# The filter of a Fourier mixing layer: loaded in pair order as float32 and cast in place, instead of permuted by matmuls

## Chip, core and metric

The kernel runs on one core of one Trainium2 chip. The metric is the device time of one execution in microseconds (us), the median of three runs. Engines are named as in the profile: PE is the matrix engine, DVE the vector engine, ACT the scalar engine, POOL the general-purpose engine (GpSimd), and SP the engine that only issues transfers. A transfer can be put on a queue by SP, by ACT or by POOL. An engine executes its own instructions in order, and waits on semaphores that other engines and transfers raise.

## What is computed

```python
X = np.fft.rfft(x, axis=1)                       # x: 8 x 3008 x 256, float32
Y = X * (filt_r + 1j * filt_i)[None]             # filters: 1505 x 256
y = np.fft.irfft(Y, n=3008, axis=1).astype(np.float32)
h = np.maximum(y.reshape(-1, 256) @ w_in, 0.0)   # w_in: 256 x 2048
out = (h * h) @ w_out                            # w_out: 2048 x 256
```

A global filter along the sequence (Fourier transform, product with a complex filter, transform back) is followed by a feed-forward layer with squared ReLU on all 24064 tokens.

## The kernel before

The transform of length 3008 is split as 64 x 47, and every step of it is a product with a constant matrix. For one batch the steps are these.

- `unit_a` (for batch 0: `chunk_a0`, L366, and `turn_u`, L388) is the transform of length 47. Batch 0 takes its rows from three wide loads `xw` (L228), cast to float16 by DVE and POOL.
- `unit_b` (L411) is the transform of length 64. It makes two columns of frequencies (`c`) at a time with the constant `sSB`, and DVE multiplies the bank by the filter: one instruction gives the product with the real and with the imaginary filter, `sF[:, v, c]` with v = 0 and 1 (L425). There are 12 such products for a batch, p = 0 to 11, and product p uses columns 2p and 2p + 1.
- `unit_p` (batch 0: `unit_p0`, L438) goes back over the 64 with the constant `sSP`, and, for batch 0, with `sSPx`, which is `sSP` with its halves of partitions swapped (POOL, L773 and L774). ACT moves the bank to `ze`, and SP writes it to `dZ` in DRAM.
- `read_z` (L476) reads it back in another order as `zt`, and `unit_y` (L484) finishes the inverse transform and leaves `yt`.
- `ffn_g1` (L512), `ffn_sq`, and `products` and `sums` (L602, L632) are the feed-forward layer, in 47 groups of 512 tokens with 8 slots each. From the first group on, the transforms of batches 1 to 7 are put in these slots by a plan written out by hand (`fft_plan`, L669). What comes ahead of the first slot is the prologue: it brings batch 0 to `yt`, and batch 1 through `unit_a`.

`sF` has 128 partitions. Partition f of column c holds frequency 47 f + c for f < 32, and 47 (f - 32) + 47 - c for f of 32 to 63; partitions 64 to 127 repeat this, with the sign changed for the imaginary filter. The kernel before loads each filter as 128 rows of 3008 numbers (`load_f`, L234), casts them to float16 in `f16` (L755 on POOL; L763 on DVE, POOL and ACT) and lets PE permute them: `place_f` (L269) multiplies slices of `f16` by 0-1 matrices `sPF` (108 matmuls in all, L284 and L287) into PSUM, and ACT copies each four columns into `sF` (L295). The last frequency is loaded apart (`nyq`, L248). Calls of `place_f` stand between the calls of `unit_b` (L780 to L789).

Each engine's order is the order of the program text. PSUM is in three rings of two buffers: `psH` (two banks each), `psF` and `psO`. In the prologue, `turn_u` and `place_f` rotate over all of them (`bank_pair`, L169).

Transfers in the prologue, in the order of SP's queue: the three `xw`, `filt_r`, `sPF`, `filt_i`, a small constant `sC1`, the two halves of `sSB` and `sSP`, seven pieces of `w_in` (`load_win`, L304), the six `dZ` writes and the first `zt` reads. POOL's queue carries the eight loads of batch 1's `x` (`load_x`, L186, which casts to float16 on the way), and `w_out` in two halves (`load_wout`, L320): the first half after the loads of `x`, the second half after the first `zt` has landed (L793). A new transfer takes one of eight semaphores in turn, and its issue waits until the transfer eight places earlier has landed.

Of the kernel before, what the change touches and what calls it, by code (L numbers as in the profile page):

```python
# [9 lines left out]
F16 = mybir.dt.float16  # L10
# [9 lines left out]
TG = 512  # L20
SLOTS = 8
CLS = 376
QF = 3008
PQ = ((0, 0), (0, 1), (0, 2), (1, 2), (1, 3), (1, 0))


def _build_consts():
# [23 lines left out]
    for c in range(NC):  # L51
        for j in range(32):
            freq[c, j] = 47 * j + c
            if c:
                freq[c, 32 + j] = 47 * j + 47 - c
    freq[0, 32] = N // 2


    SB = np.zeros((NM, 2, 2, NC, 2, 64))
# [3 lines left out]
    for c in range(NC):  # L63
        for f in range(64):
            k = freq[c, f]
            if k < 0:
                continue
            sg = 1.0 if (f < 32 or c == 0) else -1.0
            for h in range(2):
                th = 2 * np.pi * ((k * (32 * h + m)) % N) / N  # L70
                SB[:, h, 0, c, 0, f] = np.cos(th)
                SB[:, h, 1, c, 0, f] = -sg * np.sin(th)
                SB[:, h, 0, c, 1, f] = -np.sin(th)
                SB[:, h, 1, c, 1, f] = -sg * np.cos(th)
            if c == 0 and f == 32:
                SB[:, :, 1, c, :, f] = 0.0
            w = (1.0 if k in (0, N // 2) else 2.0) / N
            for i in range(2):
                th = 2 * np.pi * ((k * (n1j + i)) % N) / N
                cs, sn = w * np.cos(th), w * np.sin(th)  # L80
                SP[0, f, c, i, 0] = cs
                SP[0, f, c, i, 1] = sg * sn
                SP[1, f, c, i, 0] = -sn
                SP[1, f, c, i, 1] = sg * cs
# [7 lines left out]
            SY[c + c // 12 * 4, i, 1, :, i] = -np.sin(th)  # L92


    PF = np.zeros((128, 6, 2, 2, 32))
    for w, (s, q) in enumerate(PQ):
        for j in range(32):
            PF[4 * j + q, w, :, s, j] = 1.0

    f16 = lambda a, p: np.ascontiguousarray(a.reshape(p, -1).astype(np.float16))  # L100
    C0 = np.zeros((128, 896))
    C0[:, 0:576] = S0.reshape(128, 6, 2, 2, NC).transpose(0, 1, 4, 2, 3).reshape(128, 576)
# [1 line left out]
    for h in range(2):  # L104
        C0[64 * h:64 * h + N2, 704:752] = SA[:, h, h].reshape(N2, 48)
    C0[:, 768:862] = SY.reshape(128, 94)
    return f16(C0, 128), f16(PF, 128), f16(SB, 128), f16(SP, 128)


@with_exitstack  # L110
def kernel(
# [16 lines left out]
    NG = T // TG  # L128
    assert NG * TG == T

    C0_np, PF_np, SB_np, SP_np = _build_consts()
    dPF = nc.inline_tensor(PF_np, name="cPF")
    dC0 = nc.inline_tensor(C0_np, name="cC0")
    dSB = nc.inline_tensor(SB_np, name="cSB")
    dSP = nc.inline_tensor(SP_np, name="cSP")
# [27 lines left out]
    def psH(name):  # L163
        return pps.tile([128, 2, 512], F32, tag="psH", name=name, bufs=2)
# [37 lines left out]
    sSA = sC1[:, 0:64]  # L202
    sSY = sC1[0:112, 64:158]
    ident = sC0[:, 576:704]
    sPF = p_out.tile([128, 6, 128], F16, tag="ost", name="sPF")

    xw32, xw16 = {}, {}

# [20 lines left out]
        load_wide(k)  # L229


    f32s = []

    def load_f(im):  # L234
        filt = filt_i if im else filt_r
        t = p_y.tile([128, QF], F32, tag="yt", name=f"f32_{im}")
        nc.sync.dma_start(out=t, in_=filt[0:1504, :].rearrange("a d -> (a d)")
                          .rearrange("(p e) -> p e", e=QF))
        f32s.append(t)

    load_f(0)
    nc.sync.dma_start(out=sPF, in_=dPF.ap().rearrange("p (w q) -> p w q", q=128))
    load_f(1)
    nc.sync.dma_start(out=sC1, in_=dC0.ap()[:, 704:896])
    nyq = p_out.tile([128, 2, D], F32, tag="ost", name="nyq")
    nc.gpsimd.memset(nyq, 0.0)
    for im, filt in enumerate((filt_r, filt_i)):
        nc.gpsimd.dma_start(out=nyq[0:1, im, :], in_=filt[1504:1505, :])  # L248
    sSB = const.tile([128, NC, 128], F16, name="sSB")
    sSP = const.tile([128, NC, 128], F16, name="sSP")  # L250
    sign = const.tile([128, 1], F32, name="sign")
    nc.vector.memset(sign[0:64], 1.0)
    nc.vector.memset(sign[64:128], -1.0)


    zero = const.tile([128, 128], F16, name="zero")
    nc.vector.memset(zero, 0.0)

    nc.scalar.copy(out=zero[0:1, 0:1], in_=zero[0:1, 1:2])

    sF = const.tile([128, 2, NC, D], F16, name="sF")
    nc.vector.memset(sF[:, 0, 0:2, :], 0.0)
    ps = psO("warm").rearrange("p a d -> p (a d)")
    for _ in range(26):
        nc.tensor.matmul(ps, zero, sF[:, 0, 0:2, :], start=True, stop=True)  # L265

    f16s = []

    def place_f(im, k, *engs, rotate=False):  # L269

        if rotate:
            banks, groups = bank_pair(f"psf_{im}_{k}")
        else:
            t = psH(f"psf_{im}_{k}")
            banks, groups = [t[:, 0, :], t[:, 1, :]], [(t, 0)]
        for i in range(4):
            c = 4 * k + i
            e0, e1 = D * c, D * (47 - c)
            cuts = [0] + [d for d in range(1, D)
                          if (e0 + d) % QF == 0 or (c and (e1 + d) % QF == 0)] + [D]  # L280
            for d0, d1 in zip(cuts, cuts[1:]):
                o = banks[i // 2][:, (i % 2) * D + d0:(i % 2) * D + d1]
                q, a = divmod(e0 + d0, QF)
                nc.tensor.matmul(o, sPF[:, PQ.index((0, q)), :], f16s[0][:, im, a:a + d1 - d0],  # L284
                                 start=True, stop=False)
                q, a = divmod(e1 + d0, QF) if c else (0, QF + d0)
                nc.tensor.matmul(o, sPF[:, PQ.index((1, q)), :], f16s[0][:, im, a:a + d1 - d0],  # L287
                                 start=False, stop=True)
        for t, i in groups:
            n = t.shape[1]  # L290
            eng = engs[i % len(engs)]
            dst = sF[:, im, 4 * k + 2 * i:4 * k + 2 * i + 2 * n, :]
            src = t.rearrange("p t (a d) -> p (t a) d", d=D)
            if eng is nc.scalar:
                eng.activation(out=dst, in_=src, func=AF.Copy, scale=sign[:, 0:1] if im else 1.0)  # L295
            elif im:
                eng.tensor_scalar_mul(out=dst, in0=src, scalar1=sign[:, 0:1])
            else:
                eng.tensor_copy(out=dst, in_=src)

    sWin = const.tile([128, 2, DFF], F16, name="sWin")
    sWout = const.tile([128, NJT, 256], F16, name="sWout")
# [84 lines left out]

    def turn_u(k, eng):  # L388

        banks, groups = bank_pair(f"psT_{k}")  # L390
# [345 lines left out]
    for k in range(3):  # L736
        cast_wide(k, nc.vector, nc.gpsimd if k == 2 else nc.vector)

    def load_const(t, d, k):
        c = slice(12 * k, 12 * k + 12)  # L740
        nc.sync.dma_start(out=t, in_=d.ap().rearrange("p (a b) -> p a b", b=128)[:, c, :])

    for k in range(2):
        c = slice(12 * k, 12 * k + 12)
        load_const(sSB[:, c, :], dSB, k)
        load_const(sSP[:, c, :], dSP, k)
    load_win()
    for c in (0, 2, 1, 3):
        chunk_a0(c)
    f16s.append(p_h2.tile([128, 2, QF + D], F16, tag="h2", name="f16"))  # L750
    e0, e1 = slice(0, 1504), slice(1504, QF)
    for im in range(2):
        nc.gpsimd.tensor_copy(out=f16s[0][:, im, QF:], in_=nyq[:, im, :])
    for e in (e0, e1):
        nc.gpsimd.tensor_copy(out=f16s[0][:, 0, e], in_=f32s[0][:, e])  # L755
    uts[0] = p_ut.tile([128, NC, D], F16, tag="ut", name="ut_0")
    turn_u(0, nc.scalar)
    turn_u(1, nc.vector)
    turn_u(2, nc.scalar)
    turn_u(3, nc.vector)  # L760
    place_f(0, 0, nc.scalar, rotate=True)
    for eng, e in ((nc.vector, slice(0, 1024)), (nc.gpsimd, slice(1024, 2048)),
                   (nc.scalar, slice(2048, QF))):  # L763
        cast(eng, f16s[0][:, 1, e], f32s[1][:, e])
    turn_u(4, nc.vector)
    place_f(0, 1, nc.scalar, rotate=True)
    turn_u(5, nc.vector)
    place_f(1, 0, nc.scalar, nc.vector, rotate=True)
    for k in range(6):
        if k % 3 == 0:  # L770
            sSPx.append(p_u.tile([128, 12, 128], F16, tag="u", name=f"sSPx_{k}"))
        c, o = slice(4 * k, 4 * k + 4), slice(4 * k % 12, 4 * k % 12 + 4)
        nc.gpsimd.tensor_copy(out=sSPx[-1][0:64, o, :], in_=sSP[64:128, c, :])  # L773
        nc.gpsimd.tensor_copy(out=sSPx[-1][64:128, o, :], in_=sSP[0:64, c, :])  # L774
        if k < 4:
            load_x(1, 2 * k)
            load_x(1, 2 * k + 1)
    load_wout(0)
    cast_win()
    for k in range(7):  # L780
        if k < 6:
            unit_b(0, 2 * k)
            if k < 5:
                place_f(1, k + 1, nc.scalar)
            unit_b(0, 2 * k + 1)
        if k > 0:
            unit_p0(k - 1)
        if k < 4:
            place_f(0, k + 2, nc.scalar)  # L789
    read_z(0, 0)  # L790
    read_z(0, 1)
    tiny = const.tile([1, 1], F16, name="tiny")
    nc.gpsimd.tensor_copy(out=tiny, in_=ztiles[0][0:1, 0, 0:1])  # L793
    load_wout(1)
    for c in range(4):
        unit_a(1, c)
    ps = psF("fill")
# [62 lines left out]
```

## Time and profile before

| | |
|---|---|
| time, median of 3 | 759.16 us (757.97 to 759.77) |
| profiled execution | 757.66 us, span 755.9 us |
| busy over the span | PE 98%, DVE 87%, ACT 75%, POOL 26% |
| granted PE clock | full in all 40 slices |

The span is nearly all feed-forward groups. The change touches only the first 50 us. This is how busy the engines are there, in us of each stretch of 5 (or 10) us, with the mean share of the 16 transfer engines and what they moved:

| stretch, us | PE | DVE | ACT | POOL | transfers | GB/s |
|---|---|---|---|---|---|---|
| 5 to 10 | 5.00 | 2.48 | 0.00 | 0.00 | 1.02 | 426 |
| 10 to 15 | 5.00 | 2.80 | 1.82 | 2.34 | 1.03 | 433 |
| 15 to 20 | 4.58 | 3.15 | 3.41 | 2.80 | 0.98 | 398 |
| 20 to 25 | 5.00 | 4.76 | 4.76 | 3.46 | 1.04 | 389 |
| 25 to 30 | 4.89 | 4.95 | 4.69 | 4.80 | 1.07 | 312 |
| 30 to 35 | 4.78 | 4.00 | 4.73 | 4.81 | 1.08 | 231 |
| 35 to 40 | 4.64 | 4.06 | 4.49 | 4.52 | 1.10 | 187 |
| 40 to 45 | 3.85 | 3.74 | 3.93 | 0.00 | 1.00 | 255 |
| 45 to 50 | 4.07 | 2.02 | 1.94 | 1.07 | 0.74 | 152 |

A share of 1 means that all 16 transfer engines had a packet in hand all the time (packets of one engine overlap a little, so it can pass 1). GB/s falls from 25 us on although the share doesn't: the packets of that time are slower ones.

### The profile page before, as it was taken

The page shows a single profiled execution, that of the slowest core. Times are in us where ns is not written, and L with a number is a line of the kernel's source. Part 1 is how long each engine was busy: PE and PEld are TensorE (multiplying, and loading weights), DVE is VectorE, ACT ScalarE, POOL GpSimd, SP SyncE. Part 2 cuts the span into 40 slices and gives each one's busy share as a digit, 9 for nine tenths or more (in the row PEclk, how much of TensorE's full clock was granted, in tenths as well). Part 3 has the DMA queues.
Part 4 walks back from the last instruction along what each step waited for, and adds up shares of the span by engine and source line. Part 5 has one row for each costly group of instructions (what it writes and reads, how often), then busy time and mean ns, then how long its engine had stood idle before and what let it go on. Part 6 is the DMA issues. An engine that isn't in the chain of part 4 may idle for free.

```text
span 755.9 us, 20010 instructions
## 1 busy us (share of the span) xinstructions
PE 741.9 (98%) x8419; PEld 542.8 (72%) x8419; DVE 655.4 (87%) x730; ACT 564.2 (75%) x803; POOL 193.9 (26%) x267
## 2 busy tenths in 40 slices
PE   8988999999999999999999999999999999999998
PEld 5845766777777777877778777787678777777776
DVE  5859998899899898989979998899989989888783
ACT  2967788778878777787777778777777777777773
POOL 3811750244222321232303224033311222000000
PEclk9999999999999999999999999999999999999999
DMA  9994898666785566756586646764547333321011
GB/s 364 298 221 147 144 185 224 174 115 121 165 220 121 97 130 161 194 104 133 107 216 127 131 102 131 229 126 101 115 108 207 80 78 92 99 85 43 30 57 57
DMA packets 103026, 106.51 MB, mean 141 GB/s; under 512 B 10144, under 2 KB 93472, under 8 KB 101400
## 3 DMA queue, kind: packets, MB, share of 16 engines
q1 hardware_dynamic: 83496, 81.99, 35.7%
q0 software_dynamic: 19296, 23.05, 22.1%
q8 instruction: 66, 1.08, 0.6%
q14 instruction: 24, 0.20, 0.1%
q10 hardware_dynamic: 144, 0.18, 0.1%
HBM read 57.97 MB, written 48.23 MB: 141 GB/s over the span
## 4 chain that ended last, share of the span: by engine, by line
PE 90%; DVE 5%; ACT 2%; DMA 1%; issue 1%; ACTq 0%; DVEq 0%
PE psH L528 40%; PE psX L643 21%; PE psY L643 16%; PE psY L498 3%; PE psB L417 2%; PE psP L462 2%; PE psA L348 2%; DVE prod L425 2%; PE warm L265 1%; PE psO L548 1%; ACT h L532 1%; DVE h L539 1%; PE psf L284 1%; PE psf L287 1%; DMA prod<-prod 1%
## 5 line engine op out<-in xcount | busy, mean ns | idle before, releaser
L532 ACT ACTIVATE h<-psH 128x1024 f16<-128x1024 f32 x376 | 385.3, 1026 | 160.2 <-PE psH L528 159.2
L528 PE MATMUL psH<-yt,sWin 128*128 128x512 f16 (+7 forms) x1728 | 386.8, 351 | 1.2 <-ACT h L532 0.4
L539 DVE TENSOR_TENSOR h<-h 128x2048 f16<-128x2048 f16 (+1 forms) x192 | 229.8, 1197 | 45.5 <-ACT h L532 45.1
L432 POOL DMA_DIRECT2D prod<-prod x168 | 138.8, 967 | 428.5 <-DVE prod L425 426.1
L528 PEld LDWEIGHTS <-sWin 128*128 128x128 f16 x1728 | 149.1, 98 | 90.5 <-issue 3.0
L643 PEld LDWEIGHTS <-sum 128*128 128x128 f16 x2944 | 181.4, 98 | 26.2 <-issue 6.3
L643 PEld LDWEIGHTS <-h 128*128 128x128 f16 x2208 | 135.6, 98 | 24.5 <-issue 5.3
L425 DVE TENSOR_TENSOR prod<-psB,sF 128x1024 f16<-128x1024 f32 x84 | 102.3, 1219 | 11.9 <-PE psB L417 11.8
L643 PE MATMUL psX<-sT,sum 128*128 128x128 f16 x1472 | 104.7, 219 | 0.0
L643 PE MATMUL psY<-sT,sum 128*128 128x128 f16 x736 | 71.2, 219 | 0.0
L643 PE MATMUL psY<-sWout,sum 128*128 128x128 f16 x736 | 56.0, 219 | 1.4 <-DVE bot L658 1.4
L617 DVE TENSOR_TENSOR sum<-sum,h 128x2048 f16<-128x2048 f16 x46 | 56.1, 1220 | 0.8
L643 PE MATMUL psY<-sWout,h 128*128 128x128 f16 x736 | 56.2, 219 | 0.0
L643 PE MATMUL psX<-sT,h 128*128 128x128 f16 x736 | 56.1, 219 | 0.0
L620 DVE TENSOR_TENSOR sum<-h 128x2048 f16<-128x2048 f16 x46 | 56.0, 1217 | 0.0
L623 DVE TENSOR_TENSOR sum<-h,sum 128x2048 f16<-128x2048 f16 x46 | 55.9, 1216 | 0.0
L195 POOL DMA_DIRECT2D x<-in_x_dram x64 | 55.8, 1045 | 0.5 <-PE psA L348 0.5
L614 DVE TENSOR_TENSOR sum<-h 128x2048 f16<-128x2048 f16 x46 | 55.9, 1215 | 0.0
L464 ACT CAST ze<-psP 128x512 f16<-128x512 f32 x84 | 49.2, 585 | 1.2 <-PE psP L462 1.1
L643 PE MATMUL psX<-sWout,h 128*128 128x128 f16 x736 | 48.7, 219 | 0.0
L507 DVE CAST yt<-psY 128x376 f16<-128x376 f32 x62 | 33.7, 543 | 14.3 <-PE psY L498 14.1
L498 PE MATMUL psY<-sC,zt 112*128 112x94 f16 x512 | 42.3, 204 | 1.3 <-DMA zt<-dZ 0.9
(78 smaller groups left out, 571.3 us busy)
## 6 DMA issues: line engine op xcount, KB each, us to landing
zt<-dZ SPq DMA_DIRECT2D x64, 192.0 KB
dU<-u SPq DMA_DIRECT2D x56, 192.0 KB
prod<-prod POOLq DMA_DIRECT2D x168, 64.0 KB, 2.7
dZ<-ze SPq DMA_DIRECT2D x28, 384.0 KB
x<-in_x_dram POOLq DMA_DIRECT2D x48, 192.0 KB, 5.3
ut<-dU SPq DMA_DIRECT2D x7, 1024.0 KB
out_dram<-bot SPq DMA_DIRECT2D x32, 128.0 KB
out_dram<-top SPq DMA_DIRECT2D x16, 256.0 KB
```

What stands on the lines that cost most here:

```text
L195: nc.gpsimd.dma_start(out=t[64 * h + p0:64 * h + p1], in_=v[p0:p1, 8 * c:8 * c + 8, :])
L425: nc.vector.tensor_mul(out=prod, in0=ps.rearrange("p (a d) -> p a d", d=D).unsqueeze(1).to_broadcast([128, 2, 2, D]), in1=sF[:, :, 2 * p:2 ...
L432: nc.gpsimd.dma_start(out=prod[64 * i:64 * i + 64, 0], in_=prod[64 - 64 * i:128 - 64 * i, 1], accum_op=mybir.AluOpType.add)
L498: nc.tensor.matmul(ps[:, 94 * jj:94 * jj + 94], zt[:, 4 * (g % 2) + jj, dt * 128:(dt + 1) * 128], sSY, start=True, stop=True)
L528: nc.tensor.matmul(ps[:, i, o:o + n], sWin[:, dt, jt * 128:(jt + 1) * 128], yts[b][:, dt, r:r + n], start=(dt == 0), stop=(dt == 1))
L532: nc.scalar.activation(out=h2[:, 2 * s:2 * s + 2, :], in_=ps, func=AF.Relu)
L539: nc.vector.tensor_mul(out=v, in0=v, in1=v)
L614: nc.vector.tensor_add(out=t, in0=a21, in1=a22)
L617: nc.vector.tensor_sub(out=t, in0=f[5], in1=a11)
L620: nc.vector.tensor_sub(out=t, in0=a11, in1=a21)
L623: nc.vector.tensor_sub(out=t, in0=a12, in1=f[6])
L643: nc.tensor.matmul(o[:, t, :], f[p][:, q, 128 * t:128 * t + 128], sg["w"][p][:, q, :], start=(m == 0 and p in (1, 2)), stop=(q == 7), skip ...
```

## The change

The filters are no longer permuted on PE. They are loaded so that partition and column are already right, as float32, and only the upper half of the partitions has to be made from the lower. `sF[64:128]` is a copy of `sF[0:64]` (times -1 for the imaginary filter).

- **Loads** (`load_f(eng, v, h)`): filter v, columns 12h to 12h + 11, in two transfers of 32 partitions: one with a run of 12 KB for each partition, one with 12 runs of 1 KB in falling order. `filt_r` (v = 0) goes to partitions 0 to 63 of the float32 tile and is issued by SP; `filt_i` (v = 1) goes to partitions 64 to 127 and is issued by ACT, after a copy `junk` that waits for the second `xw`.
- **SP's queue** is now: the three `xw`, `filt_r` half 0, `sSB` and `sSP` half 0, `filt_r` half 1, `sSB` and `sSP` half 1, `sC1`, the seven pieces of `w_in`, the mirror transfer below, and then `dZ` and `zt` as before.
- **Casts** (`cast_f`) of 64 partitions: POOL does v = 1 columns 0 to 5 and v = 0 columns 6 to 23, DVE v = 0 columns 0 to 5, ACT v = 1 columns 6 to 23.
- **Mirrors** (`mirror_f`): five DVE instructions, and one transfer issued by SP for v = 0, columns 12 to 23.
- **Gone**: `place_f`, `sPF`, `sign`, `nyq` and their transfers, matmuls and bank copies.
- **Moved**: `turn_u` uses `psH` alone, all its copies are ACT's, and its calls 2 to 5 stand between those of `unit_b`; both halves of `w_out` are loaded after the first `zt` has landed.

```diff
-    load_f(0)
-    nc.sync.dma_start(out=sPF, in_=dPF.ap().rearrange("p (w q) -> p w q", q=128))
-    load_f(1)
...
+    def load_f(eng, v, h):
+
+        filt = (filt_r, filt_i)[v]
+        t = f32s[h][64 * v:64 * v + 64]
+        eng.dma_start(out=t[0:32].rearrange("p c d -> p (c d)"),
+                      in_=bass.AP(tensor=filt.tensor, offset=filt.offset + 12 * h * D,
+                                  ap=[[47 * D, 32], [1, 12 * D]]))
+        eng.dma_start(out=t[32:64],
+                      in_=bass.AP(tensor=filt.tensor, offset=filt.offset + (47 - 12 * h) * D,
+                                  ap=[[47 * D, 32], [-D, 12], [1, D]]))
...
+    def cast_f(eng, v, c0, c1):
+        h = c0 // 12
+        cast(eng, sF[0:64, v, c0:c1, :], f32s[h][64 * v:64 * v + 64, c0 - 12 * h:c1 - 12 * h, :])
+
+    def mirror_f(v, c0, c1):
+        nc.vector.tensor_scalar_mul(out=sF[64:128, v, c0:c1, :], in0=sF[0:64, v, c0:c1, :],
+                                    scalar1=-1.0 if v else 1.0)
...
+    junk = const.tile([128, 1], F32, name="junk")
+    nc.scalar.copy(out=junk, in_=xw32[1][:, 0, 0:1])
+
+    for h in range(2):
+        load_f(nc.scalar, 1, h)
+    for h in range(2):
+        load_f(nc.sync, 0, h)
+        load_const(sSB, dSB, h)
+        load_const(sSP, dSP, h)
+    nc.sync.dma_start(out=sC1, in_=dC0.ap()[:, 704:896])
...
     load_win()
     for c in (0, 2, 1, 3):
         chunk_a0(c)
...
+    cast_f(nc.gpsimd, 1, 0, 6)
+    cast_f(nc.gpsimd, 0, 6, 12)
+    swap_p(0)
+    for k in range(2):
+        load_x(1, k)
+    cast_f(nc.gpsimd, 0, 12, 18)
+    cast_f(nc.gpsimd, 0, 18, 24)
+    for k in range(1, 6):
+        swap_p(k)
         if k < 4:
             load_x(1, 2 * k)
             load_x(1, 2 * k + 1)
-    load_wout(0)
     cast_win()
+    turn_u(0, nc.scalar)
+    cast_f(nc.vector, 0, 0, 6)
+    mirror_f(0, 0, 6)
+    mirror_f(1, 0, 6)
+    turn_u(1, nc.scalar)
+    cast_f(nc.scalar, 1, 6, 12)
+    nc.sync.dma_start(out=sF[64:128, 0, 12:24, :], in_=sF[0:64, 0, 12:24, :])
     for k in range(7):
         if k < 6:
+            if k == 3:
+                mirror_f(1, 12, 24)
             unit_b(0, 2 * k)
-            if k < 5:
-                place_f(1, k + 1, nc.scalar)
+            if k == 1:
+                for v in range(2):
+                    mirror_f(v, 6, 12)
             unit_b(0, 2 * k + 1)
+        if k + 2 < 6:
+            turn_u(k + 2, nc.scalar)
         if k > 0:
             unit_p0(k - 1)
-        if k < 4:
-            place_f(0, k + 2, nc.scalar)
+        if k == 1:
+            cast_f(nc.scalar, 1, 12, 24)
...
-    load_wout(1)
+    for k in range(2):
+        load_wout(k)
```

More of the change, by code (lines that the diff above doesn't have):

```diff
@@ L22 @@
 CLS = 376
-QF = 3008
-PQ = ((0, 0), (0, 1), (0, 2), (1, 2), (1, 3), (1, 0))
 def _build_consts():
@@ L55, in _build_consts @@
                 freq[c, 32 + j] = 47 * j + 47 - c
-    freq[0, 32] = N // 2
+    freq[0, 63] = N // 2
     SB = np.zeros((NM, 2, 2, NC, 2, 64))
@@ L74, in _build_consts @@
                 SB[:, h, 1, c, 1, f] = -sg * np.cos(th)
-            if c == 0 and f == 32:
+            if c == 0 and f == 63:
                 SB[:, :, 1, c, :, f] = 0.0
@@ L92, in _build_consts @@
             SY[c + c // 12 * 4, i, 1, :, i] = -np.sin(th)
[L95 to L98, printed above, removed]
     f16 = lambda a, p: np.ascontiguousarray(a.reshape(p, -1).astype(np.float16))
@@ L106, in _build_consts @@
     C0[:, 768:862] = SY.reshape(128, 94)
-    return f16(C0, 128), f16(PF, 128), f16(SB, 128), f16(SP, 128)
+    return f16(C0, 128), f16(SB, 128), f16(SP, 128)
 @with_exitstack
@@ L129 @@
     assert NG * TG == T
-    C0_np, PF_np, SB_np, SP_np = _build_consts()
-    dPF = nc.inline_tensor(PF_np, name="cPF")
+    C0_np, SB_np, SP_np = _build_consts()
     dC0 = nc.inline_tensor(C0_np, name="cC0")
@@ L204 @@
     ident = sC0[:, 576:704]
-    sPF = p_out.tile([128, 6, 128], F16, tag="ost", name="sPF")
     xw32, xw16 = {}, {}
@@ L229, with load_const @@
         load_wide(k)
[L232 to L239, printed above, removed]
-    load_f(0)
-    nc.sync.dma_start(out=sPF, in_=dPF.ap().rearrange("p (w q) -> p w q", q=128))
-    load_f(1)
[L244 to L248, printed above, removed]
+    f32s = [p_y.tile([128, 12, D], F32, tag="yt", name=f"f32_{h}") for h in range(2)]
+    def load_f(eng, v, h):
[7 more added lines that the diff above has]
+                                  ap=[[47 * D, 32], [-D, 12], [1, D]]))
+    def load_const(t, d, k):
+        c = slice(12 * k, 12 * k + 12)
+        nc.sync.dma_start(out=t[:, c, :], in_=d.ap().rearrange("p (a b) -> p a b", b=128)[:, c, :])
+    def cast_f(eng, v, c0, c1):
[4 more added lines that the diff above has]
+                                    scalar1=-1.0 if v else 1.0)
     sSB = const.tile([128, NC, 128], F16, name="sSB")
     sSP = const.tile([128, NC, 128], F16, name="sSP")
-    sign = const.tile([128, 1], F32, name="sign")
-    nc.vector.memset(sign[0:64], 1.0)
-    nc.vector.memset(sign[64:128], -1.0)
     zero = const.tile([128, 128], F16, name="zero")
@@ L265 @@
         nc.tensor.matmul(ps, zero, sF[:, 0, 0:2, :], start=True, stop=True)
[L267 to L299, printed above, removed]
     sWin = const.tile([128, 2, DFF], F16, name="sWin")
@@ L388, in turn_u @@
     def turn_u(k, eng):
-        banks, groups = bank_pair(f"psT_{k}")
+        t = psH(f"psT_{k}")
+        banks, groups = [t[:, 0, :], t[:, 1, :]], [(t, 0)]
         for i in range(4):
@@ L737 @@
         cast_wide(k, nc.vector, nc.gpsimd if k == 2 else nc.vector)
[L739 to L746, printed above, removed]
     load_win()
@@ L749, with swap_p @@
         chunk_a0(c)
[L750 to L755, printed above, removed]
-    uts[0] = p_ut.tile([128, NC, D], F16, tag="ut", name="ut_0")
[L757 to L769, printed above, removed]
+    uts[0] = p_ut.tile([128, NC, D], F16, tag="ut", name="ut_0")
+    def swap_p(k):
         if k % 3 == 0:
```

## The prediction

> **What bounds the kernel now.** I read first the chain of waits up to 85 us. After the prologue it is matmuls and DVE work of the groups, which the change leaves alone, so only the time at which the first group starts can move. These are the links ahead of it (start, length, what):
>
> ```profile
> 38.21 2.36 DVE prods L425 x2
> 40.61 0.61 PE psP L448 x4
> 41.24 1.02 ACT ze L450
> 42.28 3.28 DMA dZ<-ze
> 45.58 3.04 DMA zt<-dZ
> ...
> 50.21 1.19 PE psH L528 x4
> ```
>
> From DVE's last product of batch 0 (end 40.57) to the first group (50.21) the order is fixed: bank, copy, write, read, inverse transform. So the question is when DVE ends its twelve products. The timeline of DVE (start, length, instruction, count, idle before) says:
>
> ```profile
> 24.62 7.02 DVE L425 TENSOR_TENSOR prods<-psB,sF 128x1024 f16<-128x1024 f32 x6 [0.24 <-issue]
> 32.60 2.36 DVE L425 TENSOR_TENSOR prods<-psB,sF 128x1024 f16<-128x1024 f32 x2 [0.96 <-ACT ze L450]
> 35.94 4.62 DVE L425 TENSOR_TENSOR prods<-psB,sF 128x1024 f16<-128x1024 f32 x4 [0.98 <-ACT ze L450]
> ```
>
> Six in a row take 7.02 us, 1.17 each. Twelve would take 14.0, but from first to last 15.95 pass: twice DVE waits for ACT, which in each period of 3.33 us copies two filter banks (rows of 1.02 and 1.11 us) and one `ze` (1.01). So PE's permutation costs little; ACT's bank copies, and the start at 24.6, cost.
>
> Then the transfers, by windows (stretch, busy times of the engines, clock, transfer share, GB/s) and by queue:
>
> ```profile
> 10.50:13.50 3.00, 3.00 (x56) 2.56 (x54) 1.32 (x3) 1.13 (x3) 2.11 (x3) 1.00 1.02 435
> 28.00:31.50 3.50, 3.39 (x35) 2.93 (x35) 3.45 (x4) 3.33 (x4) 3.42 (x7) 1.00 1.07 218
> 47.50:48.75 1.25, 0.40 (x4) 0.13 (x3) 0.00 (x0) 0.00 (x0) 0.00 (x0) 1.00 1.11 206
> ...
> q0 software_dynamic: 227, 0.70, 100.0%
> q1 hardware_dynamic: 54, 0.07, 7.0%
> ```
>
> The engines have no free time until 45 us. Loads over 128 partitions move 435 GB/s (first row). Batch 1's `x` moves 218, and while it runs, POOL's queue q0 has the engines to itself: the last two rows are the queues of 28 to 31.5 us (packets, MB, share), and q1, which is SP's, gets 7% (the view doesn't show how much it still had to move). The third row is the `zt` reads, 48 partitions each: 206.
>
> **What the Trainium skill says.** "DMA: Bandwidth & Descriptors", section Queues, rings and completion order: a transfer engine takes the descriptors of one queue in order and goes round between queues by packets. The trace agrees: `filt_r`, `filt_i` and `sSP`, queued in this order, land in this order (14.97, 20.46, 22.5, where POOL's wait for each ends). "SBUF — State Buffer", section Door 1: The DMA port swizzle: partitions 0 to 31, and 0 to 63 too, reach only 8 of 16 ports, measured 189 and 196 GB/s against 328 for all; its section on two DMAs for both halves gives only 6% more for two at once. The 206 above agrees with the first; of two halves at once the prologue shows no clean case. The new filter transfers are of this kind, 32 partitions each.
>
> **The change on the engines.** Off the path: 108 matmuls of about 0.11 us step, and ACT's banks, 11 of about 1.06 and two of 0.55, 12.8 us. ACT gets six `turn_u` banks (6.1; before it had two of six), and casts of 1536 and 3072 elements. A row `f` 128x960 took 0.985, and "ScalarE: Activation LUTs", What ACT_TABLE_LOAD costs, prices 186 ns + 0.833 ns an element: 1.47 and 2.75. DVE loses 4.8 of `turn_u` and 0.86 of cast, and gets by "VectorE: DVE Perf Modes", Side-by-side (two float32 or four 16-bit elements a cycle, 0.16 fixed): a cast of 1536, 0.96; four mirrors of 0.56; one of 3072, 0.96. POOL's four casts are 1.47 each, scaled from 128x1504 in 1.444.
>
> Suppose all data are there. `uT` ended at 17.75. ACT's new issue of its fourth transfer waits for its first to land, and the `uT` copies queue behind it on ACT; I allow 0.9 (0 to 2.5) and get 18.65. DVE: cast and two mirrors, 2.08, so the products start at 20.7. Six products and two mirrors, 8.14: 28.85. The large mirror: 29.8. Six more products, 7.05: 36.85. ACT has 2.0 us for each 2.34 of DVE, apart from the cast of 2.75, so it costs DVE at most a few tenths. By engines alone the products end 3.7 us sooner.
>
> **The change on the transfers.** Products 6 to 11 need `sF[64:128, 0, 12:24]`, which comes by SP's transfer. In SP's queue it stands behind all of `w_in`. Before, POOL first reads `w_in` at 35.2 us, so its place didn't matter. So this is the added wait: DVE at product 6, and behind it PE's banks, ACT's `ze` and everything after. When does it land? I count from the third `xw`'s landing at 11.3, which stays:
>
> - both filters' half 0, 1.57 MB: 3.7 us at 425 GB/s if the two halves of the ports complement each other, 7.6 at 206 if they don't; I take 5.2 (300 GB/s): 16.5.
> - `sSB`, `sSP` half 0 with `filt_i` half 1, 1.57 MB, mostly 128 partitions: 3.7: 20.2.
> - `filt_r` half 1, 0.79 MB, alone on its ports: 3.8 at 206 (1.85 at 425): 24.0.
> - `sSB`, `sSP` half 1 and `sC1`, 0.84 MB: 2.0: 26.0.
> - `w_in`, 2.1 MB at 425: 4.95: 30.95.
> - POOL now issues two loads of `x` as soon as `sSP` half 0 is there (about 21.5), in the middle of this. Before, eight loads held the engines for about 8 us, so two hold them for 2.0: 32.95. If they get no turn before SP's queue is empty, 0.
> - the mirror transfer, 0.39 MB from one half of the ports to the other, 1.9 at 206 (0.93 at 425): 34.85.
> - the next two loads of `x`, issued after POOL's casts of `filt_r` half 1 (24.0 + 2.9 + the swaps 1.3 = 28.2), reach the engines about 30 and take part of 2.0: I take 0.9: 35.7.
>
> So product 6 starts at 35.8 instead of 29.8, and the products end at 42.85: 2.3 us later than 40.57. With all low ends the transfer lands at 28.4 and the engines' 29.8 rules; with all high ones near 41.
>
> **After the products.** The last `dZ` write no longer shares with `w_out`; I take 0.5 off its 3.28, since the fill matmuls on PE would soon rule. Against it, `w_out` now loads 1.0 MB (of float16) instead of 0.5 beside the `dU` writes. One half took 8.8 to 9.1 us to land; two take some 15 from 3.9 ahead of the first group, so they land about 11.2 after it starts, and DVE first needs all of it (L595) 61.38 - 50.21 = 11.2 after. `zt` behind them in SP's queue is needed at 63.15. I put 0.4 on it (0 to 2). Sum: 2.3 - 0.5 + 0.4 = 2.2.
>
> **Rivals.**
> - *A, the mirror transfer is stuck behind `w_in`*: 759.2 + 2.2 = 761.4. For it: SP's queue order and a full share. Against it: I take half rates that only the 48-partition reads show. 0.38.
> - *B, the halves complement each other, `x` costs its 2.0*: 11.3 + 3.9 + 3.7 + 3.4 + 2.0 + 4.95 + 2.0 + 1.9 = 33.2, products end at 40.3, and time is 759 (757.7 to 760.7). 0.20.
> - *C, the engines rule*: filter loads at full rate and `x` waits its turn. 3.7 + 0.5 off, at most 1 back: 755.7. For it: in 10.5 to 13.5 us the engines are at 435, and the first `x` landed 7 us after issue, so it does wait. Against it: three favourable values at once. 0.30.
> - *D, half rate everywhere, and `w_out` late too*: landing at 39, 5.6 + 1: 765.5. For it: the 6% above. 0.12.
>
> **How the numbers follow.** A is likeliest: 761.4. Slower is A and D, 0.50; same is B, 0.20; faster is C, 0.30. The range leaves out about 1 in 10 at each end: below lies the better third of C, above most of D. So 755.6 to 765.0.
>
> **What will show it.** In the timeline of DVE after: first product near 20.7 (if later, ACT was held at its transfer or a cast was late); a gap ahead of the seventh product of some 6 us, ended by the `sF` transfer (no gap: C); periods of 2.34 us, not 3.33, elsewhere. In the windows: GB/s near 300 in 12 to 16 us, and near 206 for `filt_r` half 1. In the chain: first `psH` of a group at 52.4. I am wrong if the transfer lands by 30, or if DVE stands at L595.

## The result, and the profile after

The changed kernel takes 768.73 us (median of 4 runs, 766.11 to 769.99) where the kernel before takes 759.08 (4 runs, one more than in the table above): a ratio of 1.0124 with an interval of 1.0094 to 1.0154, slower by 9.65 us. The forecast was 761.4 with a range of 755.6 to 765.0. The side was right, the size was not: 2.2 us were forecast.

The profiled execution after is the longest of the four (span 768.1, before 755.9). Line numbers below are those of the changed kernel: L210 are the casts, L229 and L232 the filter transfers, L245 the mirrors, L354 and L356 the `uT` copies of ACT and DVE, L396 the products, L499 the first matmuls of a group, L566 `make_t`. First the chain of waits up to 60 us (start, length, what):

```profile
31.60 2.89 POOL sF L210 x2
...
34.50 8.15 DMA sF<-sF
...
52.15 3.17 DMA zt<-dZ
...
56.54 15.67 DMA sWout<-in_moe_w_out_dram
```

Before, matmuls and DVE stood here up to the last product, and then `dZ`, `zt` and the group's matmuls. Now transfers carry it: the mirror transfer, and behind the products the load of `w_out`. Then DVE's timeline (start, length, instruction, count, and in brackets what ended the idle time before it):

```profile
24.39 0.56 DVE L356 CAST uT<-psA 128x384 f16<-128x384 f32 x1 [0.72 <-PE psA L347]
24.86 0.94 DVE L210 CAST sF<-f 64x1536 f16<-64x1536 f32 x1
25.84 3.44 DVE L245 TENSOR_SCALAR sF<-sF 64x1536 f16<-64x1536 f16 x2
29.58 3.49 DVE L396 TENSOR_TENSOR prods<-psB,sF 128x1024 f16<-128x1024 f32 x3 [0.30 <-DMA f<-in_filt_i_dram]
33.10 2.67 DVE L245 TENSOR_SCALAR sF<-sF 64x1536 f16<-64x1536 f16 x2
35.88 3.49 DVE L396 TENSOR_TENSOR prods<-psB,sF 128x1024 f16<-128x1024 f32 x3
39.40 0.95 DVE L245 TENSOR_SCALAR sF<-sF 64x3072 f16<-64x3072 f16 x1
42.77 6.88 DVE L396 TENSOR_TENSOR prods<-psB,sF 128x1024 f16<-128x1024 f32 x6 [2.43 <-DMA sF<-sF]
```

The twelve products end at 49.65 and not at 40.57 (+9.1). They begin 5 us later than before (29.58, was 24.62), two pairs of mirrors take 3.44 and 2.67, and the gap ahead of the seventh product is there, ended by the `sF` transfer. The last row shows what the change was for: six products in 6.88, with no wait between them.

Why so late? ACT's and POOL's timelines, two rows and one, and a row of SP's waits (what it waited for, us in all, times, longest):

```profile
19.08 0.32 ACTq L232 DMA_DIRECT2D f<-in_filt_i_dram  x1
19.44 2.39 ACT L354 CAST uT<-psA 128x384 f16<-128x384 f32 x6 [10.50 <-DMA f<-in_filt_i_dram]
```

```profile
25.23 3.64 POOL L210 CAST sF<-f 64x1536 f16<-64x1536 f32 x2 [11.95 <-DMA f<-in_filt_i_dram]
```

```profile
SPq L238 <- DMA f<-in_filt_i_dram: 11.2, 1, 11.2
```

ACT's fourth filter transfer is issued at 19.08, when an earlier one of `filt_i` has landed, and the `uT` copies behind it start at 19.44 (before at 12.15). POOL's cast of `filt_i` half 0 waits until 25.23: that half, issued about 9 us, lands 16 us later. SP stands too: until 25.09 it waits for a transfer of `filt_i`, since semaphores are taken in turn, and so it issues half 1 of `sSB` and all that follows (`w_in` from 26.96) only then. The transfers themselves, in windows (stretch, busy times, clock, transfer share, GB/s) and by queue for 10 to 25 us (packets, MB, share of the 16 transfer engines):

```profile
10.50:13.50 3.00, 2.51 (x56) 2.36 (x54) 1.81 (x4) 0.00 (x0) 1.56 (x1) 1.00 1.02 203
14.00:18.00 4.00, 0.26 (x6) 0.16 (x4) 0.24 (x1) 0.00 (x0) 0.00 (x0) 0.76 0.97 206
20.00:25.00 5.00, 4.22 (x49) 3.89 (x49) 2.19 (x5) 2.79 (x7) 0.00 (x0) 0.50 1.02 242
```

```profile
q1 hardware_dynamic: 1116, 2.40, 67.0%
q10 hardware_dynamic: 571, 1.25, 37.3%
```

The transfer engines are as full as before (share about 1) but move 203 to 242 GB/s where they moved 435 in the first of these windows. SP's queue (q1) and ACT's (q10) run side by side from 10 to 25 us, and the sum is still 244. PE, with next to nothing to do from 14.3 to 20.3, has its clock granted at 0.5 in 20 to 25.

Behind the products, the first group starts at about 58.65 (before 50.21, +8.4), and DVE's first `make_t` waits for `w_out`, so it is 10.9 later than before (first the row before, where it is L595, then the row after):

```profile
61.38 0.68 DVE L595 TENSOR_TENSOR sT<-sWout 128x1024 f16<-128x1024 f16 x1
```

```profile
72.32 0.69 DVE L566 TENSOR_TENSOR sT<-sWout 128x1024 f16<-128x1024 f16 x1 [2.42 <-DMA sWout<-in_moe_w_out_dram]
```

### The profile page after: what moved, and what is told of

Read it like the earlier page. It is cut to its first block, busy times and chain, and to the rows that moved or that the text cites. A ratio compares the mean times of both kernels' runs of the same rounds, so it can differ in the third digit from the quotient of the medians.

```text
span 768.1 us, 19783 instructions
## 1 busy us (share of the span) xinstructions
PE 737.7 (96%) x8311; PEld 537.1 (70%) x8311; DVE 657.6 (86%) x727; ACT 558.7 (73%) x795; POOL 195.7 (25%) x263
## 4 chain that ended last, share of the span: by engine, by line
PE 83%; DMA 9%; DVE 5%; POOL 1%; issue 1%; SPq 0%; ACT 0%; DVEq 0%; POOLq 0%
PE psH L499 38%; PE psX L614 20%; PE psY L614 15%; DMA f<-in_filt_r_dram 3%; PE psY L469 2%; PE psP L433 2%; PE psB L388 2%; DMA sWout<-in_moe_w_out_dram 2%; PE psA L318 2%; DMA zt<-dZ 2%; DVE prod L396 1%; DMA sF<-sF 1%; DVE h L510 1%; PE psO L519 1%; DVE prods L396 1%
## 5 line engine op out<-in xcount | busy, mean ns | idle before, releaser
L499 PE MATMUL psH<-yt,sWin 128*128 128x512 f16 (+7 forms) x1728 | 386.8, 351 | 1.2 <-ACT h L503 0.4
L499 PEld LDWEIGHTS <-sWin 128*128 128x128 f16 x1728 | 149.1, 98 | 90.5 <-issue 3.0
L396 DVE TENSOR_TENSOR prod<-psB,sF 128x1024 f16<-128x1024 f32 x84 | 102.3, 1219 | 11.9 <-PE psB L388 11.8
```

Source lines behind the costliest of these rows:

```text
L396: nc.vector.tensor_mul(out=prod, in0=ps.rearrange("p (a d) -> p a d", d=D).unsqueeze(1).to_broadcast([128, 2, 2, D]), in1=sF[:, :, 2 * p:2 ...
L499: nc.tensor.matmul(ps[:, i, o:o + n], sWin[:, dt, jt * 128:(jt + 1) * 128], yts[b][:, dt, r:r + n], start=(dt == 0), stop=(dt == 1))
```

## Theories

- **H**: a filter transfer of 32 neighbouring partitions moves at half rate, two of them on the two halves of the ports do not make up for each other, and since the transfer engines have no free time until 45 us, the whole prologue ends as much later as the filter takes longer. 3.15 MB take 7.4 us at 425 GB/s and about 15 at 210, so some 7 to 8 us.
- **A**: ACT, held at its fourth issue, costs the time (`uT` late, PE's clock lower after its idle time).
- **S**: the wait for the mirror transfer costs it.
- **W**: both halves of `w_out` late cost 2.4.
- **R**, against H: the reversed rows go in runs of 1 KB, and short runs, or their order, make the loads slow.

## Experiments

**What makes the filter slow: three edits of the kernel before.** Each replaces the transfer of one filter (128 partitions of 12 KB) by four; layout, bytes and result stay. Here `src` is the filter as 128 rows of `QF` elements. In brackets behind each time stands its ratio to the kernel before, timed beside it, with the interval.

```diff
-        nc.sync.dma_start(out=t, in_=src)
+        for q in range(4):                       # 32 neighbours
+            nc.sync.dma_start(out=t[32 * q:32 * q + 32], in_=src[32 * q:32 * q + 32])
```

```diff
+        for q in range(4):                       # every fourth partition
+            nc.sync.dma_start(out=t.rearrange("(p q) e -> q p e", q=4)[q],
+                              in_=src.rearrange("(p q) e -> q p e", q=4)[q])
```

```diff
+        for q in range(4):                       # 128 partitions, runs of 752 bytes
+            nc.sync.dma_start(out=t.rearrange("p (a b e) -> p b a e", b=4, e=188)[:, q],
+                              in_=src.rearrange("p (a b e) -> p b a e", b=4, e=188)[:, q])
```

> The kernel before with each filter loaded in four transfers of 32 partitions in place of one of 128; the runs stay at 12 KB a partition, the layout and the bytes are the same. Theory H (the span of partitions sets the rate): f_r lands at about 18.7 instead of 14.97, f_i at about 27.9 instead of 20.46, each 12-KB packet takes twice as long, the first product comes near 32 instead of 24.6, and the time is 764 to 767. Rival (the 1-KB runs of the reversed rows are what made the loads slow): nothing changes, 759.2 within 1. Rival (halves of the ports complement each other, since all four transfers are queued at once): f_i lands by 22, and the time is within 2 of 759.2.

> The kernel before with each filter in four transfers of 32 partitions, as in the run that gave 767.43, but each takes every fourth partition (q, q + 4, q + 8, ...) and not 32 neighbours: the same number of transfers, partitions, packets and bytes. If it matters which partitions a transfer reaches (the Trainium skill, SBUF — State Buffer, section Door 1, has every fourth partition reach all 16 ports and 32 neighbours reach 8): f_r lands near 15, f_i near 20.5, time 759.2 within 1. If the number of partitions in a transfer matters: f_i near 28, time 766 to 768.

> The kernel before with each filter loaded in four transfers of 128 partitions, each of them in runs of 752 bytes (every fourth run of a partition's 12 KB), same layout and bytes. Theory H (span of partitions): f_i lands within 1 us of 20.5, and the time is 759.2 within 1. Rival (short runs make the loads slow, at twice the time per byte): f_r lands near 18.7, f_i near 28, and the time is 764 to 767.

Measured: 767.43 with 32 neighbours (1.0109, 1.0094 to 1.0124), 759.11 with every fourth (1.0001, 0.9988 to 1.0013), 761.09 with runs of 752 bytes (1.0024, 1.0008 to 1.004). The windows of 32 neighbours, and below them those of every fourth partition:

```profile
15.00:20.00 5.00, 3.18 (x56) 2.72 (x52) 3.89 (x7) 2.95 (x5) 0.77 (x1) 1.00 1.03 218
20.00:25.00 5.00, 3.38 (x24) 2.75 (x25) 0.16 (x1) 1.02 (x1) 2.06 (x2) 0.77 1.00 211
```

```profile
15.00:20.00 5.00, 4.58 (x78) 4.20 (x76) 3.83 (x7) 3.20 (x7) 2.83 (x2) 1.00 0.99 401
20.00:25.00 5.00, 5.00 (x56) 4.30 (x54) 4.68 (x6) 4.96 (x7) 3.68 (x5) 1.00 1.03 404
```

The number of transfers, packets and bytes is the same: 218 and 211 GB/s against 401 and 404. With 32 neighbours POOL has `filt_i` at 27.96 and the products start at 31.02; with every fourth at 20.88 and 23.93. So it is which partitions a transfer reaches, as H says, and this alone, in the kernel before, makes 8.3 us (767.43 against 759.11), where the whole change makes 9.65. Short runs are ruled out as the main cause, though not as a cost: those of 752 bytes moved 336 GB/s in 10 to 20 us, and cost 1.6 (761.09 against 759.49 of the kernel before beside it), 0.9 more than H allowed. The falling order of the rows is taken up at the one-queue run.

**Do the two halves make up for each other?** The kernel before with partitions 0 to 63 on SP's queue and 64 to 127 on ACT's.

```diff
+        nc.sync.dma_start(out=t[0:64], in_=src[0:64])
+        nc.scalar.dma_start(out=t[64:128], in_=src[64:128])
...
+    nc.scalar.copy(out=junk, in_=xw32[1][:, 0, 0:1])
```

> The kernel before with each filter in two transfers at once: partitions 0 to 63 by SP's queue, 64 to 127 by ACT's (issued behind the second xw, as in the changed kernel). If two halves in two queues complement each other, filt_i lands within 1 us of 20.5 and the time is 759.2 within 1. If they do not at all, filt_i lands near 28 as with four transfers in one queue, time 766 to 767.5. At the 242 to 248 GB/s that the changed kernel's trace shows while both queues are busy: filt_i lands near 24, time 762 to 764.

Measured: 767.02 (1.0095, 1.0075 to 1.0115). The time itself says little: the copy `junk`, which lets ACT issue behind the second `xw`, stands ahead of the one that PE's first matmuls (26 on a constant, without use of their result) wait for, so PE began its real work at 17.87. The rate can be read all the same (windows):

```profile
12.00:16.00 4.00, 4.00 (x15) 1.61 (x14) 0.62 (x1) 0.00 (x0) 2.27 (x3) 1.00 0.99 222
16.00:20.00 4.00, 4.00 (x58) 2.94 (x57) 0.49 (x2) 0.99 (x3) 0.00 (x0) 1.00 1.01 248
```

222 and 248 against 211 and 218 of one half at a time: a sixth more at best, not twice (some of `sPF`, which reaches all 128 partitions, may be in these windows). The Trainium skill, "SBUF — State Buffer", section "Can I just issue two DMAs to hit both halves?", has 6% more; the runs agree that it is little.

**ACT's issues behind its `uT` copies** (theory A), in the changed kernel:

```diff
-    for h in range(2):
-        load_f(nc.scalar, 1, h)
+    load_f(nc.scalar, 1, 0)
...
     for c in (0, 2, 1, 3):
         chunk_a0(c)
+    load_f(nc.scalar, 1, 1)
```

> The changed kernel with ACT issuing the two transfers of filt_i half 1 after its uT copies, so that no copy stands behind the wait of a fourth transfer. Theory H (transfers of 32 partitions run at about half rate, and the two queues do not complement each other, so filt_i half 0 lands at about 25): uT is done near 18 instead of 25 and the clock holds in 15 to 20 us, but POOL's cast of filt_i half 0 still starts near 25, the first product comes at 28 to 29.5 instead of 29.58, and the time falls by 0 to 2 us, to 767 to 769. Theory A (ACT held at its issue is what costs): the first product comes near 22, and the time falls by about 7, to 761.5.

Measured: 768.03 (1.0114, 1.0097 to 1.0131), 0.7 below the changed kernel and inside its spread. DVE's timeline:

```profile
15.59 2.00 DVE L355 CAST uT<-psA 128x384 f16<-128x384 f32 x4 [0.78 <-PE psA L346]
...
19.45 0.55 DVE L245 TENSOR_SCALAR sF<-sF 64x1536 f16<-64x1536 f16 x1
27.26 0.55 DVE L245 TENSOR_SCALAR sF<-sF 64x1536 f16<-64x1536 f16 x1 [7.26 <-POOL sF L210]
29.17 3.48 DVE L395 TENSOR_TENSOR prods<-psB,sF 128x1024 f16<-128x1024 f32 x3 [1.36 <-DMA sSB<-cSB]
```

`uT` is done at 17.6, seven microseconds sooner, and next to nothing comes of it: the mirror of `filt_i` waits for POOL until 27.26, as POOL's cast starts at 25.76. While the loads are slow, A is ruled out as a cause of its own.

**One queue, no added waits, and then the partitions.** In the changed kernel all filter transfers go to SP's queue (the copy `junk` goes with ACT's) and DVE mirrors what SP's transfer mirrored. Then the same with each transfer over 128 partitions of 3 KB.

```diff
-    for h in range(2):
-        load_f(nc.scalar, 1, h)
     for h in range(2):
         load_f(nc.sync, 0, h)
+        load_f(nc.sync, 1, h)
...
-    nc.sync.dma_start(out=sF[64:128, 0, 12:24, :], in_=sF[0:64, 0, 12:24, :])
...
+                mirror_f(0, 12, 24)
                 mirror_f(1, 12, 24)
```

```diff
+        for i in range(2):
+            c = 6 * v + 3 * i
+            eng.dma_start(out=f32s[h][:, c:c + 3], in_=...)   # [[3 * D, 128], [1, 3 * D]]
```

> The changed kernel with all filter transfers in SP's queue (filt_r half 0, filt_i half 0, sSB and sSP half 0, then the same of half 1), so ACT issues none of them, and with the mirror of filt_r's columns 12 to 24 made by DVE in place of the transfer: the two added waits are gone, the half rate stays. Theory H with a rate of 205 GB/s: filt_r half 0 lands at 15.2, filt_i half 0 at 19.1, sSB and sSP half 0 at 21, first product near 22; filt_i half 1 at 28.8, its cast on ACT to 31.6, so product 6 at about 33, products end at 40, time 758.5 to 761. Rival (w_out late costs 2.4 in any version of the changed kernel): 762. Rival (the loads of x and w_in that come on top make it late all the same): over 764.

> The run with one queue and no added waits, with each filter transfer (384 KB) spread over 128 partitions, 3 KB each; the rows are not in pair order, so the placing of the filter is left out, the casts read as many elements as before. Only the partitions of the loads differ from the one-queue run (767.17; first product at 23.04, product 6 at 35.90, zt waited for until 55.68). Theory H (the half rate adds about 8 us of transfer time ahead of the first group, and this sets the end whatever the order): filters' half 0 lands near 15.5, half 1 near 21, w_in near 28; first product near 20, product 6 near 31.7, products end near 38.6, time 756.5 to 760. Rival (the engines' part of the change, casts and mirrors, or the clock lost by an idle PE costs the rest): 762 or more.

Measured: 767.17 (1.0093, 1.0068 to 1.0118), and over 128 partitions 758.04 (0.9987, 0.9977 to 0.9997). The windows of the first, then of the second:

```profile
12.00:20.00 8.00, 5.23 (x105) 4.77 (x102) 5.47 (x11) 5.33 (x9) 1.66 (x2) 1.00 1.06 227
20.00:28.00 8.00, 5.76 (x44) 4.86 (x45) 5.38 (x7) 3.56 (x4) 5.25 (x7) 0.58 1.08 218
```

```profile
12.00:20.00 8.00, 6.92 (x136) 6.47 (x133) 6.58 (x12) 5.38 (x10) 5.46 (x5) 1.00 1.03 405
20.00:28.00 8.00, 4.02 (x41) 2.93 (x39) 7.21 (x9) 6.61 (x6) 7.79 (x11) 1.00 1.06 329
```

The pair differs in the loads alone and by 9.1 us: H for the second time, now in the changed kernel. With the partitions the runs differ too: 3 KB, where the loads over 32 partitions have 12 KB, or 1 KB in falling order. But falling order is no slower here: in the one-queue run SP issues at 13.46, 15.41, 17.31 and 19.30 us, each time when the next of the first four filter transfers has landed. The first and the third have runs of 12 KB, the second and the fourth rows of 1 KB in falling order, and the steps are 1.95, 1.90 and 1.99 us for 0.39 MB each, 198 to 207 GB/s.

The one-queue run missed its expectation (758.5 to 761), and the way it missed teaches most. Its products do end at 43.38, six microseconds before those of the changed kernel, but the time falls by 1.6 only, and the two spreads overlap. Its chain:

```profile
47.74 4.55 DMA dZ<-ze
...
52.42 3.12 DMA zt<-dZ
...
58.38 2.92 PE psH L496 x7
```

From the last product to the first group 14.4 us pass (57.77 - 43.38) and not 9.6. The last `dZ` write was issued at 47.74, 2.7 us after its bank was copied (45.08; in the kernel before it follows at once). The profile puts this wait down to ACT's copies of `u`, which `dZ` doesn't read; a late transfer of `w_in` is likelier, since SP had waited 2.7 us for `w_in` before and POOL waits for it until 45.98, but this isn't shown. The write then took 4.55 against 3.28 before, and PE, idle for 5 us, came back at half clock: seven `psH` in 2.92, 0.42 each, where the kernel before took 1.04 for its second four. So with slow loads, taking the two waits away made DVE early, not the group.

**The changed kernel with loads over 128 partitions only** (both added waits left in; rows out of pair order as above).

> The changed kernel with each filter transfer (384 KB) spread over all 128 partitions, 3 KB each, in place of 32 partitions of 12 KB. The casts read as many elements from the same tiles, but the rows are not in pair order: the placing of the filter is left out. Everything else, also ACT's fourth issue and the mirror transfer, stays. Theory H (span of partitions): the four half-0 transfers land by about 15.5, ACT is let go at 14, uT is done by 20, the first product comes near 22.5 instead of 29.58, the mirror transfer lands by 33 instead of 42.65, products end near 39 to 40, time 757.5 to 761. Rival (the waits that the change adds, ACT's fourth issue and the mirror behind w_in, cost most in themselves): over 764.

Measured: 764.61 (1.0085, 1.0052 to 1.0117), but from 761.27 to 768.81, a spread that neither kernel has. The median misses what H expects (757.5 to 761) and lies where the rival stands (over 764). The profiled execution is the fastest, 761.27:

```profile
21.53 3.48 DVE L397 TENSOR_TENSOR prods<-psB,sF 128x1024 f16<-128x1024 f32 x3 [1.36 <-POOL sF L210]
...
31.14 1.02 DVE L246 TENSOR_SCALAR sF<-sF 64x3072 f16<-64x3072 f16 x1
35.93 6.88 DVE L397 TENSOR_TENSOR prods<-psB,sF 128x1024 f16<-128x1024 f32 x6 [3.77 <-POOL sSPx L721]
```

The first product is 8 us sooner, as H expects, and then DVE stands for 3.77 us. The chain puts the mirror transfer there, issued at 27.13 and 8.68 us under way, and the products end at 42.81 and not at 39 to 40. In the run over 128 partitions above this wait (S) is gone.

So there are two causes, and they don't add up. By the medians the added waits cost 6.6 us with fast loads (764.61 against 758.04) and 1.6 with slow ones (768.73 against 767.17). The half rate costs 9.1 without the waits (767.17 against 758.04) and 4.1 with them (768.73 against 764.61). The half rate alone brings most of the loss, and fast loads alone would not have saved the changed kernel. How much of the 6.6 is the mirror transfer and how much ACT's hold was not run apart. Why the other executions took up to 7 us more isn't shown: only the fastest has a trace. Their mean clock was lower (0.986 to 0.993, against 0.996).

**`w_out`** (theory W), in the kernel before:

```diff
-    load_wout(0)
     cast_win()
...
-    load_wout(1)
+    for k in range(2):
+        load_wout(k)
```

> The kernel before with both halves of w_out loaded where it loaded the second alone, as the changed kernel does. Theory W (two halves at that place land too late): DVE's first make_t waits about 2.4 us for sWout, and the time is 760.5 to 762. My prediction's size for it was 0.4 (0 to 2), less up to 0.5 for a faster last dZ. Rival (the load is hidden): 758.5 to 759.5.

Measured: 758.12 (0.9985, 0.9975 to 0.9995), slightly faster. DVE does wait for it (DVE's timeline), but by half a microsecond:

```profile
60.82 0.69 DVE L595 TENSOR_TENSOR sT<-sWout 128x1024 f16<-128x1024 f16 x1 [0.54 <-DMA sWout<-in_moe_w_out_dram]
```

DVE's first work on the first group starts 1.2 us sooner (52.20, was 53.38); that `w_out` no longer shares the transfer engines with the `dZ` writes would explain it, but was not tested alone. So late `w_out` alone costs nothing in the kernel before. In the changed kernel DVE waits 2.42 there, in the one-queue run over 128 partitions 1.77 (put down to a `dU` write, of batch 1's `u` to DRAM); what moving it back is worth there wasn't measured by itself. This is the one run with nothing left out that beat both kernels, the kernel before by 0.15%.

**Sharing ACT's bank copies with DVE**, in that last kernel:

```diff
+            if len(engs) > 1:
+                groups = [(t[:, 0:1], 0), (t[:, 1:2], 1)]
...
-                place_f(1, k + 1, nc.scalar)
+                place_f(1, k + 1, nc.scalar, nc.vector)
```

> The kernel before with w_out as in the run on w_out, and with DVE copying the second half of each of the five filt_i banks that ACT copied alone (512 of 1024 elements). If ACT's bank copies set the period of 3.33 us in the twelve products, as my reading of the kernel before has it, ACT needs 2.6 and DVE about 2.95 in each, products end 1.5 to 2 us earlier than in the run on w_out (40.14), and the time is 756 to 757. Rival (PE, or transfers behind the products, set it): 758.1 within 0.6, as in the run on w_out.

Measured: 761.87 (1.003, 1.002 to 1.004), some 3.5 slower than without. In DVE's timeline the period has grown from 3.33 to 3.7:

```profile
33.93 1.23 DVE L427 TENSOR_TENSOR prods<-psB,sF 128x1024 f16<-128x1024 f32 x1 [0.21 <-PE psB L419]
35.53 0.75 DVE L299 TENSOR_SCALAR sF<-psf,sign 128x512 f16<-128x512 f32 x1 [0.37 <-ACT sF L297]
36.20 1.21 DVE L427 TENSOR_TENSOR prods<-psB,sF 128x1024 f16<-128x1024 f32 x1
37.63 1.22 DVE L427 TENSOR_TENSOR prods<-psB,sF 128x1024 f16<-128x1024 f32 x1 [0.22 <-PE psB L419]
```

DVE's half copy (0.75) waits for PE and ACT, and the product behind it waits too. Both expectations missed. This run leaves open whether ACT set the period; it only shows that a copy put between two products binds DVE to the banks. That the period falls when `place_f` goes, its matmuls and its copies together, is shown by the changed kernel itself (six products in 6.88).

**Can pair order be kept?** POOL's queue loads the filter straight into `sF[0:64]` as float16; there are no casts, DVE mirrors. Then the same with SP's loads of half 1 of `sSB` and `sSP` and of `w_in` held until DVE has mirrored half 0, and `w_out` as in the kernel before. Neither leaves anything out of the result.

```diff
+        nc.gpsimd.dma_start(out=sF[0:32, v, c, :], in_=...)    # 12 KB runs of float32
+        nc.gpsimd.dma_start(out=sF[32:64, v, c, :], in_=...)   # reversed rows of 1 KB
```

```diff
+    nc.vector.memset(sSB[:, 12:13, 0:2], 0.0)                  # behind the two mirrors
+    load_const(sSB, dSB, 1)
+    load_const(sSP, dSP, 1)
+    load_win()
```

> The one-queue run with the filter loaded by POOL's queue straight into sF in pair order as float16 (the transfer converts, as the loads of w_out do), so that half the bytes are written and no engine casts anything; DVE mirrors all. If the bytes written to half of the ports set the rate (205 GB/s): each half of both filters takes 3.8 us instead of 7.7, the first product comes near 20, products end near 37 to 39, time 755.5 to 760, at or below the kernel before. If such packets take their time by the piece (w_out's pieces, written as 512 bytes, took about 65 ns each in the kernel before, 126 GB/s): the filter takes 12.5 us in all, time 759 to 763. If they are slower still, over 764.

> The run with converting loads (763.87; filt_r half 0 landed for DVE at 19.56, filt_i half 0 at 24.23, while SP's queue loaded all of sSB, sSP and w_in beside them), with two edits: SP's loads of sSB and sSP half 1 and of w_in wait until DVE has mirrored half 0 of both filters, and the first half of w_out is loaded before the casts of w_in again, as in the kernel before. If the share that SP's queue took is what made the converting loads late (0.39 MB in 4.7 us at 56% of the engines' time is 2.65 us alone): filt_i half 0 is mirrored near 18.5, the first product comes near 19, products end near 37 instead of 43.2, DVE doesn't wait for w_out, time 754 to 757, below both kernels. If the converting packets are slow by themselves: first product after 21, time 759 to 763.

Measured: 763.87 (1.0068, 1.0045 to 1.0091) and 762.22 (1.0043, 1.0026 to 1.006): better than the changed kernel, worse than the kernel before. In the second, first a row of DVE's timeline, then its chain:

```profile
30.31 6.88 DVE L390 TENSOR_TENSOR prods<-psB,sF 128x1024 f16<-128x1024 f32 x6
```

```profile
38.91 6.82 DMA dZ<-ze
...
51.82 1.45 PE psH L493 x3
```

The products end at 37.2, as expected, 3.4 us before those of the kernel before; and the time was not 754 to 757. The last `dZ` write takes 6.82 us. While it runs, POOL's queue moves 0.52 MB, the half of `w_out` that was put back ahead of it, and SP's queue 0.96 MB, with the `dZ` writes before it, which came behind the `w_in` that was made to wait (SP's queue had the transfer engines to itself from 30 to 35 us). Then PE waits 4.6 us for `zt`, until 49.13, and comes back at a low clock (0.48 a `psH`). In the first of the two runs, where all of `w_out` comes later, only 8.9 us pass from the last product to the first group, against 14.0 here; the two edits of the second run were not tried apart. As in the one-queue run, an earlier last product did not give an earlier group.

## Why the prediction was right and wrong

**Right.** Slower, by transfers at half rate. Of the rivals the nearest is D (half rate everywhere and `w_out` late, to which I gave 0.12), not A; its sum, 759.2 + 5.6 + 1, is 765.8 and not 765.5. The products alone run at 1.15 to 1.17 each. The seventh product waits for the `sF` transfer. The tail from the last product to the first group is shorter by 0.65 (0.5 was taken). The section Door 1 of "SBUF — State Buffer", which gave the half rate, holds here in both directions: 32 neighbours 211 to 218 GB/s, every fourth partition 401 to 404.

**Wrong, the step that failed: the first one of the transfers.** It took 5.2 us (300 GB/s) for half 0 of both filters, so that they would have landed at 16.5. POOL got `filt_i` half 0 at 25.23, 8.7 later. Two errors are in it. The halves do not make up for each other (203 to 248 GB/s), so the high end, 7.6, was the value, and 18.9 the landing. And the list counted as if the queues followed each other in my order; in fact the transfers of ACT's queue shared the transfer engines with all that SP had queued behind `filt_r` (1.25 and 2.40 MB in 10 to 25 us), so ACT's half 0 came near the end of what I had listed up to 24.0.

**Wrong, the hold of ACT.** 0.9 (0 to 2.5) was taken; `uT` ended at 24.95 instead of 17.75, 7.2 later. It is the same step once more, since ACT waits for the landing of a transfer that I took to be quick. It cost little here, because POOL's cast was as late (768.03 without it). That SP would be held for 11.2 us by the same transfers was not in the list at all.

**Wrong, the mirrors.** 0.56 each by the price; the four small ones took 6.11 together. In the trace the price holds when POOL does nothing (0.55 at 19.45 in the run with ACT's issues late) and not when POOL is already casting (1.71 and 1.81 between 25.84 and 29.28, while POOL's row runs from 25.23 to 28.87). "SBUF — State Buffer", section Who interferes with whom, says it: DVE, in a mode that uses two ports, and GpSimd share a pair of ports, and who comes first keeps it for the whole instruction. The trace agrees, also in the other direction: the mirror at 27.26 in the run with ACT's issues late comes ahead of a POOL cast and takes 0.55, and that cast takes 1.85 where one alone takes 1.46. I had used the price without asking who else runs.

**Right in kind, wrong in its reason, the mirror transfer.** It was to stand behind `w_in` and land at 35.7. It was issued at 34.50, since SP waited for POOL's last cast, and took 8.15 in full transfer engines, beside the loads of `x` (0.78 MB in that time), so it landed at 42.65. The gap was 2.43 and not 6, as DVE was late itself.

**Wrong, `w_out`.** 0.4 (0 to 2) was taken, and DVE stood for 2.42, just outside; standing there at all was named as a sign of being wrong. The kernel before with the same late load waits 0.54, so the rest belongs to the changed kernel; why is open.

**Doubtful, a reading of the kernel before.** I read that PE's permutation costs little and that ACT's bank copies cost. In the chain of the kernel before, the matmuls of `place_f` (L284 and L287) make 48% of the time from 24.6 to 40.6 us and ACT's copies into `sF` 21%, and PE is busy for 9.76 of the 10 us from 27.9 to 37.9. So PE set the period at least as much as ACT. The forecast for the products themselves didn't suffer: 7.05 for the last six, and 6.88 measured.

Put together, product by product: first product 29.58 instead of 20.7 (+8.9), six products and two mirrors 9.8 instead of 8.14 (+1.65), the gap 2.4 instead of 6.0 (-3.55), the last six 6.88 instead of 7.05 (-0.2): 6.8 later than 42.85, which is 49.65. The gap that came out smaller than forecast hid a part of the miss. Then -0.65 instead of -0.5, and 2.4 at `w_out` instead of 0.4. Some 1.3 us of the profiled span come later still and are not traced to one wait.

**Too narrow, the frame.** "So the question is when DVE ends its twelve products." In the changed kernel this held: from the last product to the first group 9.0 us pass, before 9.6. In other versions it did not: 14.4 in the one-queue run, 14.0 in the last. I had read that the transfer engines have no free time until 45 us, and then counted only the transfers that DVE waits for. The short sum would have been nearer: 3.15 MB at 210 instead of 425 GB/s are 7.6 us more in a stretch that has none to spare, and five kernels with slow loads (767.0 to 768.7, whatever waits they had) lie 7.9 to 9.7 above the kernel before beside them. It is an estimate and not the whole account: the waits alone, with fast loads, lost 5.8 (764.61 against 758.83 beside it).

## What to carry to other kernels

Where a stretch keeps the transfer engines full, price a change first by the time that all its transfers take of the transfer engines, and then by the path of the one that is awaited. Reordering moved the wait in two runs here; only `w_out` could be held back at no cost. Look at which partitions a load touches: 32 neighbours moved half of what every fourth partition did. And before a price of DVE is used, look at what POOL does at that moment.

## What was not expected of the hardware

- Every fourth partition in four transfers of 32 is as fast as one transfer of 128 (759.11 against 758.76, 401 to 404 GB/s).
- A DVE mirror of 64x1536 takes 0.55 us alone and up to 1.81 when POOL is already casting.
- After some 5 to 6 us without work PE's clock was granted at 0.5 in the next 5 us (20 to 25 in the changed kernel; 55 to 60 in the one-queue run, 0.42 a `psH` matmul instead of 0.26). There a late transfer was paid for twice.
- Transfers that convert to float16 wrote 1.01 MB in 6 us with their queue at 109% of the transfer engines' time (12 to 18 us of the last run), 168 GB/s of float16. So they bring the filter sooner than float32 at half rate: at this rate its 1.57 MB of float16 take 9.4 us by estimate, against 15 for 3.15 MB at 210 GB/s.
